# A chunk's two halves on the two halves of the partitions, back and front in one TensorE visit, and the norm on 128x512

## The chip, the core and the metric

The kernel runs on one core of a Trainium2 chip. The metric is device microseconds of one execution, the median of three. TensorE is called PE in the profile (its weight loads PEld), VectorE DVE, ScalarE ACT, GpSimd POOL, and SyncE, which issues all the DMAs, SP.

## The reference

Three layers follow one another. The first is a gated linear attention over 4 batches, 8 heads and 768 positions with a decay per position; written by chunks it is

```python
cum = np.cumsum(log_a, axis=-1)
L = np.exp(cum[..., :, None] - cum[..., None, :]) * causal
M = np.einsum('bhin,bhjn->bhij', Cc, Bc) * L          # scores with decay
y = M @ xc + (Cc @ state) * np.exp(cum)[..., None]
state = decay_full * state + sum_j(Bc x xc * decay_from_j)
```

Its output, 3072 tokens of 256 columns, goes through two MLPs. The first begins with a norm over the 256 columns, the second has no norm:

```python
rms = np.sqrt(np.mean(x * x, axis=-1, keepdims=True) + 1e-06)
xn = x / rms * rms_g
x = (silu(xn @ w_gate) * (xn @ w_val)) @ w_out        # d_ff 1536
h = x @ w_in
out = (h * np.clip(h + 3, 0, 6) / 6) @ w_out2         # d_ff 2048
```

All of it is in float32; a product of the MLPs is made of three passes over high and low parts.

## The kernel before

The time axis is cut into 24 chunks (`k`) of 128 tokens of one batch, each of two halves of 64. Four chunks make a block of 512 tokens, and there are six blocks (`j`). Phase A runs the first MLP over the blocks, 12 steps `f` for each: a step's `hidden` fills two PSUM banks (`hps`, six matmuls of 128x512 each), `gate` (ACT) and `prod` (DVE) make `p`, `gh` (ACT) and `gl` (mostly POOL) split it, and `result` adds six matmuls to `acc`. Phase B does the same for the second MLP, 16 steps for each block with one `hps` bank. Attention chunks of block j+1 and its norm are put between the steps of block j (`AT` says behind which). The first four chunks stand ahead of everything.

For a chunk, DMAs bring `cb` (its B, C and x with zeros between), `L` and `P`; DVE's scan turns `L` into the decay matrix. PE then comes three times: `score` and `grow` (`sps` at L394 and L412), later `inner` (L457 and L463), later `mean` (L482). Between them DVE makes `SM` and the states `V`, ACT the squares `sq` and the copy `xT`. `mean` sums squares with a column of ones, so that a chunk's 128 sums stand on 128 partitions; `norm` takes the inverse root of 128x4 numbers on DVE and `back` spreads them over the partitions by matmuls against `eye` (`rps`, L533). `scale` multiplies `xT` by it, and `split` makes `xh` and `xl`, which the steps read.

PSUM has eight banks: two for `acc`, and three tiles of two banks (`ps_w`, tag `w`). A step takes one such tile; a chunk holds two of them from `score` to `mean`. For the first four chunks PE spreads the decays (`spread_a`, `aps`) instead of a DMA.

No engine's order is written by hand. `Plan` collects the pieces with a cost for each engine, buffer counts and priorities, and prints a fixed order for every queue; each engine then runs its queue in that order and waits on semaphores. `P.fill` puts idle matmuls on PE in gaps of its plan before the first step.

## Time and profile before

| | before |
|---|---|
| median of three runs | 679.15 us (677.57 to 680.35) |
| profiled execution, first to last instruction | 677.3 us |
| mean granted PE clock, as a share of full speed | 0.992 |
| PE busy | 657.6 us, 97% |
| DVE, ACT, POOL busy | 301.0, 298.2, 282.7 us |

Only the span of the profiled execution is on record, not a time of its own; the median of the runs is 1.85 us above that span. Matmuls overlap, so that busy time on PE is not work at full rate.

### The profile page before, as it was taken

How to read it: one execution, taken by the hardware profiler on the slowest of the kernel's cores; microseconds unless marked ns; L12 is line 12 of the kernel's file. 1: busy time of each engine (PE TensorE's matmuls, PEld its weight loads, DVE VectorE, ACT ScalarE, POOL GpSimd, SP SyncE). 2: the span in 40 equal slices, each digit the busy share in tenths (PEclk: the TensorE clock that was granted, in tenths of full speed). 3: DMA queues.
4: the chain of work that ended last, by engine and by line, in shares of the span. 5: the costliest groups of instructions: out<-in, count | busy, mean ns of one | idle time of the engine just before them, and what ended most of it. 6: DMA issues, size and time to landing. Idle time of an engine off the chain costs nothing.

```text
span 677.3 us, 10507 instructions
## 1 busy us (share of the span) xinstructions
PE 657.6 (97%) x4188; PEld 529.0 (78%) x4188; DVE 301.0 (44%) x507; ACT 298.2 (44%) x494; POOL 282.7 (42%) x239
## 2 busy tenths in 40 slices
PE   8978999999999999999999999999999999999997
PEld 7856777778778778877867777888888888888886
DVE  4799853352234334332578773232322322332222
ACT  1576632322333223313366654445454545445543
POOL 3354453333433332432232435455454545545443
PEclk9888999999999999999999999999999999999999
DMA  5995203210221123030023420000000000000000
GB/s 196 318 320 188 95 1 95 70 55 20 91 67 44 56 65 100 1 118 1 0 94 125 142 76 0 1 0 32 1 0 32 0 32 0 1 32 0 32 0 32
DMA packets 24465, 42.92 MB, mean 63 GB/s; under 512 B 2112, under 2 KB 15712, under 8 KB 24416
## 3 DMA queue, kind: packets, MB, share of 16 engines
q1 hardware_dynamic: 24416, 42.25, 19.2%
q8 instruction: 33, 0.54, 0.3%
q14 instruction: 16, 0.13, 0.1%
HBM read 38.90 MB, written 3.34 MB: 62 GB/s over the span
## 4 chain that ended last, share of the span: by engine, by line
PE 80%; DVE 10%; ACT 3%; issue 3%; DMA 2%; POOL 1%; SPq 0%; POOLq 0%; ACTq 0%; DVEq 0%
PE hps L643 41%; PE acc L643 30%; DVE cv L608 2%; PE sps L394 2%; PE sps L463 2%; DMA L<-azero 1%; DVE cv L603 1%; DVE p L679 1%; ACT p L671 1%; PE sps L457 1%; PE sps L482 1%; DVE yT L608 1%; POOL gl L242 1%; PE sps L412 1%; PE aps L359 1%
## 5 line engine op out<-in xcount | busy, mean ns | idle before, releaser
L242 POOL TENSOR_TENSOR gl<-p,gh 128x512 fp32r<-128x512 f32 x160 | 214.3, 1341 | 239.8 <-ACT gh L686 233.1
L686 ACT CAST gh<-p 128x512 fp32r<-128x512 f32 x168 | 104.5, 622 | 94.7 <-PE acc L643 92.0
L681 DVE SCALAR_TENSOR_TENSOR p<-p,hps 128x512 f32<-128x512 f32 x96 | 65.9, 687 | 170.1 <-ACT p L673 170.1
L643 PE MATMUL hps<-xh,w1h 128*128 128x512 f32 x288 | 96.3, 416 | 7.9 <-ACT p L671 4.8
L673 ACT ACTIVATE p<-hps,half 128x512 f32<-128x512 f32 x96 | 66.3, 691 | 83.8 <-POOL gl L242 82.9
L679 DVE TENSOR_TENSOR p<-p,hps 128x512 f32<-128x512 f32 x72 | 49.3, 685 | 97.7 <-PE hps L643 75.8
L643 PE MATMUL hps<-xh,w1l 128*128 128x512 f32 x288 | 90.2, 395 | 0.0
L643 PE MATMUL hps<-xl,w1h 128*128 128x512 f32 x288 | 89.9, 393 | 0.0
L643 PE MATMUL acc<-gh,w2h 128*128 128x512 f32 x192 | 74.7, 389 | 0.0
L643 PE MATMUL acc<-gh,w2l 128*128 128x512 f32 x192 | 74.7, 389 | 0.0
L643 PE MATMUL acc<-gl,w2h 128*128 128x512 f32 x192 | 74.7, 389 | 0.0
L671 ACT ACTIVATE p<-hps 128x512 f32<-128x512 f32 x72 | 43.0, 597 | 64.6 <-POOL gl L242 33.2
L643 PEld LDWEIGHTS hps<-xh,w1h 128*128 128x128 f32 x288 | 50.0, 190 | 24.6 <-ACT p L671 8.9
L643 PEld LDWEIGHTS hps<-xh,w1l 128*128 128x128 f32 x288 | 54.6, 189 | 12.4
L643 PEld LDWEIGHTS hps<-xl,w1h 128*128 128x128 f32 x288 | 54.6, 190 | 12.3
L643 PE MATMUL hps<-xh,w2h 128*128 128x512 f32 x192 | 59.6, 391 | 1.5 <-DVE p L679 0.8
L643 PE MATMUL hps<-xl,w2h 128*128 128x512 f32 x192 | 59.2, 389 | 0.0
L643 PE MATMUL hps<-xh,w2l 128*128 128x512 f32 x192 | 59.1, 389 | 0.0
L643 PE MATMUL acc<-gh,w1h 128*128 128x512 f32 x144 | 59.0, 410 | 0.0
L643 PE MATMUL acc<-gl,w1h 128*128 128x512 f32 x144 | 56.3, 391 | 0.0
L643 PE MATMUL acc<-gh,w1l 128*128 128x512 f32 x144 | 56.2, 390 | 0.0
L242 POOL TENSOR_TENSOR bh<-cb,L 128x256 f32<-128x256 f32 x24 | 17.1, 713 | 76.4 <-PE sps L412 48.3
(94 smaller groups left out, 814.3 us busy)
## 6 DMA issues: line engine op xcount, KB each, us to landing
cb<-comb SPq DMA_DIRECT2D x20, 576.0 KB, 8.1
raw<-w SPq DMA_DIRECT2D x16, 512.0 KB, 3.4
L<-azero SPq DMA_DIRECT2D x40, 128.0 KB, 3.3
yT<-w SPq DMA_DIRECT2D x6, 768.0 KB, 9.2
rawx<-w SPq DMA_DIRECT2D x6, 768.0 KB, 9.7
...
```

Of the source, the lines that this page charges most:

```text
L242: eng[e].tensor_tensor(out=out, in0=a, in1=b, op=op)
L359: pe.matmul(out=ps[64 * q:64 * q + 64, p * CH:(p + 1) * CH], rhs=az[:, q], lhsT=eye[:96, c:c + 1].to_broadcast([96, SC]), start=True, stop ...
L394: pe.matmul(out=bank2(ws[p // 2], "sps")[:, p % 2, c * SC:(c + 1) * SC], lhsT=cb[r, BN + c * 128:BN + (c + 1) * 128], rhs=cb[r, CT + c * S ...
L412: pe.matmul(out=v()[32 * p:32 * p + 32, 1, 384 + 64 * c:448 + 64 * c], lhsT=b[:, h], rhs=cb[:, 64 * (4 * c + p):64 * (4 * c + p) + 64], st ...
L463: pe.matmul(out=o[p][c], lhsT=cb[:, q:q + 64], rhs=SM[:, p, SC * c:SC * c + SC], start=False, stop=True, skip_group_check=True)
L608: dve.scalar_tensor_tensor(out=u, in0=T[kr].bitcast(I32)[:, :, 1], scalar=-0x80000000, in1=u, op0=ALU.bitwise_and, op1=ALU.bitwise_or)
L643: pe.matmul(out=o, lhsT=a, rhs=c, start=first and i == 0, stop=last and i == len(seq) - 1)
L671: act.activation(out=p[:, :n], in_=T["w", hid][:, 0, :n], func=AF.Silu)
L673: act.activation(out=p[:, :n], in_=T["w", hid][:, 0, :n], func=AF.Relu, scale=1.0 / 6.0, bias=half)
L679: dve.tensor_tensor(out=p, in0=p, in1=h, op=ALU.mult)
L681: dve.scalar_tensor_tensor(out=p, in0=p, scalar=1.0, in1=h, op0=ALU.min, op1=ALU.mult)
L686: act.copy(out=t[:, :n], in_=T["p", i][:, :n])
```

## The change

It rewrites the attention, the norm and the places of both.

- Layout. The two halves of a chunk stand on partitions 0 to 63 and 64 to 127. `score` has a weight tile of 32 rows by 64 columns and 128 moving columns, 8 matmuls as before; `grow` one of 64 by 32; the product of `SM` and x is 16 matmuls of 64 by 32 instead of 8 of 128 by 64; the product of the state and C keeps its shape. `cb` is 896 columns wide instead of 1152.
- Visits. `visit(k)` issues `score` and `grow` of chunk k and `inner` of chunk k-1 in one piece, with a drain ahead of the state's matmuls. `decay` is one DVE instruction of 512 columns instead of two of 256; `mask` (`um`, 128x128 out of PSUM) is new, and the states are made from it.
- Squares. ACT and POOL split them into `sqh` and `sql`, and `mean` multiplies them by a 128x128 matrix of ones, so that the sums stand on all partitions: four matmuls of 128x512 for a block; `mean` for each chunk and `back` are gone. `norm` works on 128x512 in SBUF, with one ACT instruction, two for the first guess and nine Newton instructions on DVE. For the first block it works chunk by chunk on 128x128 with a root.
- PSUM. Attention has four banks of its own (`ps_at`), the hidden layer two single banks (`h`), and four (`hb`) from step 9 of block 4 on, when attention is over. Before, steps and chunks shared three pairs.
- Start. `L` of the first four chunks comes by DMA from `ablk` and is clipped on POOL; `spread_a` is gone. `P.fill` begins only behind the last of the four chunks' pieces.

Cut to its core:

```diff
-AT = {0: 0, 2: 1, 4: 2, 6: 3, 8: 4}
...
+AT = [1, 3, 5, 7]
+AT_NORM = 8
+NCB = 3
...
+        if k < B:
+            P.op(dma(262144), ld_L, w=[("L", k)], boost=bst)
+            P.op({"DVE": d2(512) + 70, "POOL": 900}, clip, r=[("L", k)], w=[("L", k)], boost=bst)
+            P.op(dma(262144), lambda e: ld_cb(e, 0, XX), w=[("cb", k, 0)], boost=bst)
+            P.op(dma(196608), lambda e: ld_cb(e, XX, CW), w=[("cb", k, 1)], boost=bst)
...
-        def spread_a(e):
-            T["aps", k] = ps = ps_acc.tile([128, 512], F32, tag="acc1", name="aps")
-            for p in range(4):
-                for q in range(2):
-                    c = 4 * k + p
-                    pe.matmul(out=ps[64 * q:64 * q + 64, p * CH:(p + 1) * CH], rhs=az[:, q],
-                              lhsT=eye[:96, c:c + 1].to_broadcast([96, SC]),
-                              start=True, stop=True, skip_group_check=True)
...
-        def score(e):
-            cb = T["cb", k]
-            for c in range(2):
-                for p in range(4):
-                    r = slice(32 * p, 32 * p + 32)
-                    pe.matmul(out=bank2(ws[p // 2], "sps")[:, p % 2, c * SC:(c + 1) * SC],
-                              lhsT=cb[r, BN + c * 128:BN + (c + 1) * 128],
-                              rhs=cb[r, CT + c * SC:CT + (c + 1) * SC],
-                              start=True, stop=True, skip_group_check=True)
...
+    def score(k):
+        cb, o = T["cb", k], part(k, 0, 128)
+        for c in range(2):
+            for p in range(4):
+                r = slice(32 * p, 32 * p + 32)
+                pe.matmul(out=o[64 * c:64 * c + 64, p],
+                          lhsT=cb[r, BN + c * SC:BN + (c + 1) * SC],
+                          rhs=cb[r, CP + c * CH:CP + (c + 1) * CH],
+                          start=True, stop=True, skip_group_check=True)
...
+    def grow(k):
+        cb, b, o = T["cb", k], flat(T["bh", k]), part(k, 192, 64)
+        for p in range(4):
+            for c in range(1 if k >= NK - B else 2):
+                r = slice(64 * c, 64 * c + 64)
+                pe.matmul(out=o[32 * p:32 * p + 32, c], lhsT=b[r, 32 * p:32 * p + 32],
+                          rhs=cb[r, XX + 64 * p:XX + 64 * p + 64],
+                          start=False, stop=True, skip_group_check=True)
...
+    def inner(k, apart=False):
+        cb, SM, y = T["cb", k], T["SM", k], part(k, 128, 64)
+
+        def intra(t):
+            for g in range(4):
+                for c in range(2):
+                    h, r = 4 * t + g, slice(64 * c, 64 * c + 64)
+                    pe.matmul(out=y[32 * g:32 * g + 32, 2 * t + c], rhs=SM[r, h],
+                              lhsT=cb[r, XX + D * h:XX + D * h + D],
+                              start=False, stop=True, skip_group_check=True)
+
+        intra(0)
+        intra(1)
+        if apart:
+            pe.drain()
+        for c in range(1 if k < B else 0, 2):
+            for p in range(4):
+                r, q = slice(32 * p, 32 * p + 32), p % 2 * 64
+                pe.matmul(out=y[q:q + 64, p // 2 * 2 + c], lhsT=before(k, c)[r, :],
+                          rhs=T["ch", k][r, SC * c:SC * c + SC],
+                          start=False, stop=True, skip_group_check=True)
...
+    def mean(o, j, cols):
+        n = 0
+        for s in ("sqh", "sql"):
             for t in range(2):
...
+                pe.matmul(out=o, lhsT=ones, rhs=T[s, j][:, t, cols], start=n == 0, stop=n == 3,
+                          skip_group_check=True)
+                n += 1
...
+        def a(e):
+            v, y, z = (t[:, cols] for t in rn(j))
+            dve.scalar_tensor_tensor(out=z, in0=v, scalar=-0.5, in1=y, op0=ALU.mult, op1=ALU.mult)
+
+        def b(e):
+            v, y, z = (t[:, cols] for t in rn(j))
+            two(e, z, z, y, ALU.mult)
+
+        def c(e):
+            v, y, z = (t[:, cols] for t in rn(j))
+            dve.scalar_tensor_tensor(out=y, in0=z, scalar=1.5, in1=y, op0=ALU.add, op1=ALU.mult)
+
+        v, y, z = keys
+        P.op({"DVE": d1(n)}, a, r=[v, y], w=[z], boost=bst)
+        P.op({"DVE": d1(n)}, b, r=[z, y], w=[z], boost=bst)
+        P.op({"DVE": d1(n)}, c, r=[z, y], w=[y], boost=bst)
...
+        P.op({"PE": 600}, lambda e: mean(m(), 0, cols),
+             r=[("sq", 0, k, 0), ("sq", 0, k, 1)], w=[s + (0,)], boost=bst)
+        P.op({"DVE": d1(128)}, shift, r=[s + (0,)], w=[v], boost=bst)
+        P.op({"ACT": a1(128)}, root, r=[v], w=[z], boost=bst)
+        P.op({"DVE": d1(128) + 100}, invert, r=[z], w=[y], boost=bst)
+        newton(0, cols, (v, y, z), None, None, bst, 128)
+        for t in range(2):
+            P.op({"DVE": d1(128)}, lambda e, t=t: scale(e, 0, t, cols),
...
+        def total(e):
+            T["h", hn] = t = mlp[1].tile([128, 512], F32, tag="h", name="rps")
+            mean(t, j, cols)
+
+        def shift(e):
+            act.activation(out=rn(j)[0], in_=T["h", hn], func=AF.Copy, scale=1.0 / DM, bias=1e-6)
...
+            v, y, z = rn(j)
+            dve.tensor_scalar(out=z.bitcast(I32), in0=v.bitcast(I32), scalar1=1, scalar2=None,
                               op0=ALU.logical_shift_right)
...
+            dve.tensor_scalar(out=y.bitcast(I32), in0=z.bitcast(I32), scalar1=-1.0,
+                              scalar2=float(0x5F3759DF), op0=ALU.mult, op1=ALU.add)
+
+        P.op({"PE": 908}, total, r=[("sq", j, i, u) for i in range(B) for u in range(2)],
+             w=[("h", hn)], boost=bst)
+        P.op({"ACT": a1(512)}, shift, r=[("h", hn)], w=[v], boost=bst)
+        P.op({"DVE": d2(512) + d1(512)}, guess, r=[v], w=[y, z], boost=bst)
+        for _ in range(3):
+            newton(j, cols, (v, y, z), None, None, bst, 512)
...
+    def open1(e):
+        early.close()
+        mlp.append(ctx.enter_context(tc.tile_pool(name="ps_acc", bufs=1, space=PSUM)))
+        mlp.append(ctx.enter_context(tc.tile_pool(name="ps_h", bufs=2, space=PSUM)))
...
     def open2(e):
         att.close()
+        mlp.append(ctx.enter_context(tc.tile_pool(name="ps_hb", bufs=4, space=PSUM, side="right")))
...
+    nstep, prev, late = [0], [], []
...
-        xk = [("x", b, t, u) for t in range(2) for u in range(2)]
-        hid, nv = nxt(nw), 2 if A else 1
+        xk, nv = xkeys[b], 2 if A else 1
+        hs = [("hb", nxt(nhb)) if late else ("h", nxt(nh)) for v in range(nv)]
...
         def hidden(e, v):
-            ps = bank2(hid, "hps")[:, v]
+            ps = hid(hs[v])
...
+    for k in range(B):
+        load(k)
+        r, w = front_keys(k)
+        free = [("xT", 0, k - 2), ("q", k - 2)] if k >= 2 else []
+        P.op({"PE": 700}, lambda e, k=k: score(k), r=r[:1] + free, w=w[:1], boost=BOOST0)
+        P.op({"PE": 500}, lambda e, k=k: grow(k), r=r + w[:1], w=w[1:], boost=BOOST0)
+        middle(k)
+        r, w = back_keys(k)
+        P.op({"PE": 1000}, lambda e, k=k: inner(k), r=r, w=w, boost=BOOST0)
+        finish_chunk(k)
+        norm_chunk(k, 0)
...
+    def visit(k):
+        new, old = k < NK, k > B
+        r, w = [], []
+        if new:
+            load(k)
+            r, w = front_keys(k)
+        if old:
+            ro, wo = back_keys(k - 1)
+            r, w = r + ro, w + wo
+
+        def go(e):
+            if new:
+                score(k)
+                grow(k)
+            if old:
+                inner(k - 1, new)
```

How it moves instructions shows in three places. The first is PE in block 1 of phase A, around one chunk; `sps` is the attention's PSUM. Before:

```order
L394 MATMUL sps<-cb 128x64 x8
L412 MATMUL sps<-cb,bh 32x64 x8
L643 MATMUL hps<-xh,w1h_77 128x512 x2
L643 MATMUL hps<-xh,w1l_89 128x512 x2
L643 MATMUL hps<-xl,w1h_77 128x512 x2
L457 MATMUL sps<-ch,V 64x64 x4
L457 MATMUL sps<-ch,V_1266 64x64 x4
L463 MATMUL sps<-SM,cb 64x64 x8
L643 MATMUL acc<-gh,w1h_83 128x512
```

And now, around a visit of the same block:

```order
L705 MATMUL acc<-gl,w1h_73 128x512
L384 MATMUL sps<-cb 64x128 x8
L395 MATMUL sps<-cb,bh 32x64 x8
L410 MATMUL sps<-SM,cb 32x64 x16
L421 MATMUL sps<-ch,V 64x64 x4
L421 MATMUL sps<-ch,V_1672 64x64 x4
L705 MATMUL acc<-gh,w1h_74 128x512
```

Before, L482's two matmuls follow five rows further down, behind the six of this `acc`. Three visits (L394 with L412, L457 with L463, L482) with MLP groups between them have become one, with 8 more matmuls of `SM`.

The second is DVE in the same block, around the norm of the next one; `z`, `y` and `v` are the norm's tiles and `rps` is PSUM. Before, the last six of eleven instructions on four columns and what follows:

```order
L525 SCALAR_TENSOR_TENSOR z_1205<-v_1203,rps 128x4
L526 TENSOR_TENSOR z_1205<-z_1205,rps 128x4
L527 SCALAR_TENSOR_TENSOR rps<-z_1205,rps 128x4
L525 SCALAR_TENSOR_TENSOR z_1205<-v_1203,rps 128x4
L526 TENSOR_TENSOR z_1205<-z_1205,rps 128x4
L527 SCALAR_TENSOR_TENSOR y_1204<-z_1205,rps 128x4
L679 TENSOR_TENSOR p<-p,hps 128x512
L539 SCALAR_TENSOR_TENSOR xT<-xT,gs,rps 128x512 x2
L248 CAST xh<-xT 128x512
L242 TENSOR_TENSOR xl<-xT,xh 128x512
```

Now, from the same place on:

```order
L519 SCALAR_TENSOR_TENSOR z_1764<-v_1762,y_1763 128x512
L234 TENSOR_TENSOR z_1764<-z_1764,y_1763 128x512
L527 SCALAR_TENSOR_TENSOR y_1763<-z_1764,y_1763 128x512
L519 SCALAR_TENSOR_TENSOR z_1764<-v_1762,y_1763 128x512
L234 TENSOR_TENSOR z_1764<-z_1764,y_1763 128x512
L746 TENSOR_TENSOR p<-p,hps 128x512
L527 SCALAR_TENSOR_TENSOR y_1763<-z_1764,y_1763 128x512
L536 SCALAR_TENSOR_TENSOR xT<-xT,gs,y_1763 128x512 x2
L441 TENSOR_TENSOR SM<-sps,L 128x512
L234 TENSOR_TENSOR xl<-xT,xh 128x512
L746 TENSOR_TENSOR p<-p,hps 128x512
```

The eleven instructions have 512 columns each, one `prod` (`p`) stands behind ten of them, and another behind `scale`, `SM` and `xl`.

The third is DVE at the start, where the weights of the first MLP (`yT` 128x768) are first put together. Before:

```order
L603 SCALAR_TENSOR_TENSOR yT<-yT 128x768
L488 TENSOR_SCALAR v_324<-sps 128x1 x2
L608 SCALAR_TENSOR_TENSOR yT<-yT 128x768
L520 RECIPROCAL rps<-rps 128x4
L525 SCALAR_TENSOR_TENSOR z_326<-v_324,rps 128x4
L526 TENSOR_TENSOR z_326<-z_326,rps 128x4
L527 SCALAR_TENSOR_TENSOR y_325<-z_326,rps 128x4
L539 SCALAR_TENSOR_TENSOR xT<-xT,gs,rps 128x512 x2
L242 TENSOR_TENSOR xl<-xT,xh 128x512
L603 SCALAR_TENSOR_TENSOR yT<-yT 128x768
```

Now:

```order
L527 SCALAR_TENSOR_TENSOR y_330<-z_331,y_330 128x128
L519 SCALAR_TENSOR_TENSOR z_331<-v_329,y_330 128x128
L536 SCALAR_TENSOR_TENSOR xT<-xT,gs,y_330 128x128
L234 TENSOR_TENSOR z_331<-z_331,y_330 128x128
L536 SCALAR_TENSOR_TENSOR xT<-xT,gs,y_330 128x128
L527 SCALAR_TENSOR_TENSOR y_330<-z_331,y_330 128x128
L536 SCALAR_TENSOR_TENSOR xT<-xT,gs,y_330 128x128 x2
L240 CAST xh<-xT 128x2x128
L234 TENSOR_TENSOR xl<-xT,xh 128x2x128
L659 SCALAR_TENSOR_TENSOR yT<-yT 128x768 x2
L664 SCALAR_TENSOR_TENSOR yT<-yT 128x768 x2
```

The first weights stood ahead of the first block's norm and stand behind its last instruction now.

## Rows read from the trace of the kernel before

**Rows 1.** The page's head and its first part, TensorE's line.

```profile
span 677.3 us, 10507 instructions
PE 657.6 (97%) x4188; PEld 529.0 (78%) x4188; DVE 301.0 (44%) x507; ACT 298.2 (44%) x494; POOL 282.7 (42%) x239
```

**Rows 2.** Line L643 alone, stretches: length, PE busy (count), granted clock, DMA share, GB/s.

```profile
31.20:60.00 28.80, 18.07 (x66) 0.94 0.95 297
60.00:84.00 24.00, 17.20 (x61) 0.93 0.35 107
209.10:271.50 62.40, 53.39 (x216) 1.00 0.20 60
333.60:410.00 76.40, 72.66 (x307) 1.00 0.28 97
410.00:677.30 267.30, 262.96 (x1159) 1.00 0.03 12
```

**Rows 3.** Stretches: length; PE, PEld, DVE, ACT, POOL busy; clock, DMA share, GB/s.

```profile
0.00:31.20 31.20, 28.08 (x371) 24.76 (x372) 18.18 (x43) 10.79 (x20) 10.50 (x22) 0.95 0.77 249
31.20:60.00 28.80, 23.84 (x209) 17.78 (x207) 27.20 (x31) 18.26 (x28) 16.57 (x12) 0.94 0.95 297
209.10:271.50 62.40, 62.29 (x498) 49.28 (x497) 23.32 (x52) 18.83 (x35) 21.89 (x21) 1.00 0.20 60
```

**Rows 4.** Timeline of PE: one chunk's two visits, later the norm's broadcast.

```profile
227.02 0.67 PE L394 MATMUL sps<-cb 32*128 32x64 f32 x16
227.62 0.43 PE L412 MATMUL sps<-cb,bh 128*32 128x64 f32 x16
227.99 0.73 PE L643 MATMUL hps<-xh,w1h 128*128 128x512 f32 x2
229.57 0.46 PE L457 MATMUL sps<-ch,V 32*64 32x64 f32 x16
229.96 0.69 PE L463 MATMUL sps<-SM,cb 128*64 128x64 f32 x16
230.57 0.50 PE L643 MATMUL acc<-gh,w1h 128*128 128x512 f32 x1
232.07 0.50 PE L482 MATMUL sps<-ones,sq 128*128 128x1 f32 x4
232.43 0.49 PE L643 MATMUL acc<-gh,w1h 128*128 128x512 f32 x1
...
270.76 1.05 PE L533 MATMUL rps<-eye,y 128*128 128x128 f32 x8
271.56 0.71 PE L643 MATMUL hps<-xh,w1h 128*128 128x512 f32 x2
```

**Rows 5.** Groups of instructions: DVE on 4 and on 256 columns.

```profile
L525 DVE SCALAR_TENSOR_TENSOR z<-v,rps 128x4 f32<-128x4 f32 x16 | 2.5, 157 | 0.5
L403 DVE TENSOR_TENSOR SM<-sps,L 128x256 f32<-128x256 f32 x48 | 18.1, 416 | 0.5 <-PE sps L394 0.4
```

**Rows 6.** Timeline of DVE, then of POOL, 340 to 346 us.

```profile
340.14 0.69 DVE L608 SCALAR_TENSOR_TENSOR cv<-raw,cv 128x512 int32<-128x512 int32 x1
...
344.33 1.73 DVE L608 SCALAR_TENSOR_TENSOR cv<-raw,cv 128x512 int32<-128x512 int32 x1
...
344.22 1.29 POOL L242 TENSOR_TENSOR w2l<-cv,w2h 128x512 fp32r<-128x512 f32 x1 [4.67 <-ACT w2h L246]
```

**Rows 7.** Timeline of PE, then of ACT: behind a group, and its gate.

```profile
259.50 0.62 PE L643 MATMUL hps<-xh,w1h 128*128 128x512 f32 x2
...
259.76 0.60 ACT L671 ACTIVATE p<-hps 128x512 f32<-128x512 f32 x1 [1.02 <-PE hps L643]
```

**Rows 8.** Timeline of the start: DVE twice, then PE.

```profile
22.88 0.95 DVE L603 SCALAR_TENSOR_TENSOR yT<-yT 128x768 int32<-128x768 int32 x1
...
29.55 0.69 DVE L242 TENSOR_TENSOR xl<-xT,xh 128x512 fp32r<-128x512 f32 x1
...
31.23 0.71 PE L643 MATMUL hps<-xh,w1h 128*128 128x512 f32 x2
```

More of the change, by code (lines that the diff above doesn't have):

```diff
@@ L156, in run @@
         if self.fill:
-            fn, ns, t, cold, until = self.fill
+            fn, ns, after, cold, until = self.fill
+            t = 1 + next(s for s, i, _, _ in out if i == after)
+            cold += t
             for s, i, _, pe in sorted(o for o in out if o[3] is not None):
@@ L399, in decay @@
-        def decay(e, t):
-            if ("SM", k) not in T:
-                T["SM", k] = ap2.tile([128, 4, CH], F32, tag="SM", name="SM")
-            q = slice(2 * t, 2 * t + 2)
-            dve.tensor_tensor(out=T["SM", k][:, q], in0=T["w", ws[t]][:, :, 0:CH], op=ALU.mult,
-                              in1=T["L", k].rearrange("j (p c) i -> j p (c i)", c=2)[:, q])
-        def grow(e):
-            cb, b = T["cb", k], T["bh", k]
-            for c in range(1 if last else 2):
-                for p in range(4):
-                    h = 2 * p + c
-                    pe.matmul(out=v()[32 * p:32 * p + 32, 1, 384 + 64 * c:448 + 64 * c],
-                              lhsT=b[:, h],
-                              rhs=cb[:, 64 * (4 * c + p):64 * (4 * c + p) + 64],
-                              start=True, stop=True, skip_group_check=True)
@@ L480, in mean @@
-        def mean(e):
-            for t in range(2):
-                pe.matmul(out=v()[:, 0, 384:385], lhsT=T["sq", j][:, t, i * CH:(i + 1) * CH],
-                          rhs=ones[:, 0:1], start=t == 0, stop=t == 1, skip_group_check=True)
-        def keep(e):
-            if ("rn", j) not in T:
-                T["rn", j] = [ap1.tile([128, B], F32, tag=n, name=n) for n in ("v0", "y0", "z0")]
-            dve.tensor_scalar(out=T["rn", j][0][:, i:i + 1], in0=v()[:, 0, 384:385],
-                              scalar1=1.0 / DM, scalar2=1e-6, op0=ALU.mult, op1=ALU.add)
@@ L491, in attention @@
-        P.op({"PE": 700 if first else 1000}, inner,
-             r=[("SM", k, 0), ("SM", k, 1), ("cb", k, 0), ("cb", k, 1), ("V1", k), ("ch", k)] + vold, w=y, boost=bst)
-        if not last:
-            P.op({"DVE": 210}, lambda e: state(e, 1), r=[("V1", k), ("P", k)] + u,
-                 w=[("V", k)], boost=BOOST)
-        P.op({"ACT": a1(256)}, square, r=y, w=[("sq", j, i)], boost=bst)
-        P.op({"ACT": a1(256), "DVE": d1(256)}, evac, r=y, w=[("xT", j, i)], boost=bst)
-        P.op({"PE": 550}, mean, r=[("sq", j, i)], w=[("w", ws[0], 4)], boost=bst)
@@ new lines, in scale, with norm_chunk @@
+    def scale(e, j, t, cols):
+        x = T["xT", j][:, t, cols]
+        dve.scalar_tensor_tensor(out=x, in0=x, scalar=gs[:, t:t + 1], in1=rn(j)[1][:, cols],
+                                 op0=ALU.mult, op1=ALU.mult)
+    def norm_chunk(k, b):
+        s, bst, cols = place(k)[0], BOOST0, slice(k * CH, k * CH + CH)
+        m = lambda: part(k, 0, 128)[:, 0]
+        v, y, z = (("rn", 0, k, n) for n in range(3))
+        def shift(e):
+            dve.tensor_scalar(out=rn(0)[0][:, cols], in0=m(), scalar1=1.0 / DM, scalar2=1e-6,
@@ L531, in back @@
-        def back(e):
-            for q in range(B):
-                pe.matmul(out=T["w", wn][:, 1, q * CH:(q + 1) * CH], start=True, stop=True,
-                          lhsT=T["rn", j][1][:, q:q + 1].to_broadcast([128, 128]),
-                          rhs=eye)
-        def scale(e, t):
-            x = T["xT", j][:, t]
-            dve.scalar_tensor_tensor(out=x, in0=x, scalar=gs[:, t:t + 1], in1=T["w", wn][:, 1],
-                                     op0=ALU.mult, op1=ALU.mult)
-        wn = nxt(nw)
@@ L747, in block_kernel @@
                 lambda f: yflat[:, 4608 + f % 2 * 768:5376 + f % 2 * 768], w1h, w1l)
+    def visit(k):
[13 more added lines that the diff above has]
+                inner(k - 1, new)
+        P.op({"PE": 1500 if new and old else 950}, go, r=r, w=w, boost=BOOST)
+        if old:
+            finish_chunk(k - 1)
+        if new:
+            middle(k)
     for j in range(NB):
```

399 lines of the change are left out of this document (205 added, 194 removed).

## Prediction

> **What bounds the kernel now.** I read the page's head first: PE is busy for 97% of the span [rows 1]. A busy PE is not a PE at its peak, so the second view is the MLP's own matmuls by stretch. In phase B they run without a break: 262.96 us for 1159 of them, 0.2269 us each [rows 2], and six of them, a group, take 1.36 us. The program has 72 steps of 18 and 96 of 12, together 2448, which is 555.5 us. The other 121.8 us of the span are what this change can touch. Three kinds of stretch hold most of them. Up to 31.2 us PE does no MLP work. From 31.2 to 84 it does 66 + 61 of these matmuls [rows 2], 28.8 us of 52.8. In a steady block, 209.1 to 271.5, the 216 matmuls need 49.0 us of 62.4, so 13.4 us are attention, norm and waiting. There are four such blocks (the attention that stands in blocks 1 to 4; that in block 0 falls in the start). From 333.6 to 410, where the second MLP's weights are prepared, 307 matmuls need 69.7 us of 76.4: 6.7 are lost. Phase B loses nothing and keeps its work.
>
> In the steady block PE is busy for 62.29 of 62.4 us, DVE for 23.32 and POOL for 21.89 [rows 3]: PE is the limit, and what leaves its queue there leaves the time. In the start DVE is: it is busy for 27.20 us of the 28.8 from 31.2 on, against 18.18 of the first 31.2 [rows 3].
>
> **PE in a steady block.** From start to start [rows 4] a chunk's first visit takes 0.97 us (227.02 to 227.99), the second 1.00 (229.57 to 230.57), `mean` 0.36, together 2.33, and the norm's `back` 0.80. Each return to the MLP costs more than its own matmuls: the group from 227.99 to 229.57 took 1.58 us instead of 1.36, the one from 230.57 to 232.07 took 1.50, so 0.18 each in the mean. 4 x 2.33 + 0.80 + 13 x 0.18 = 12.5 of the 13.4; 0.9 is waiting.
>
> What a visit costs now I take from the four kinds of matmul in [rows 4], each of 16 instructions. On four tiles of 128x32 and of 32x64 they start 23 and 24 ns apart (0.37 and 0.39 us), on two tiles of 128x64 or four of 32x128 38 ns (0.61, 0.60).
> - `score`: 16 instructions on 32x64 tiles, with twice the moving columns. 0.39 us if the columns don't count, 0.78 if they do; I take 0.50, nearer the first, since half the weight columns go.
> - `grow`: 64x32, 0.37 as now, 0.61 at worst.
> - `SM` times x: 32 instructions of 64x32, 0.77 at 24 ns, 1.22 at 38. I take 0.77, as four tiles of 32 columns do that now.
> - state times C: unchanged, 0.39.
> - the drain: no row has one. Nothing, or as much as a return with its refill, 0.22; I take 0.10.
>
> That is 2.13 us (1.92 to 3.22) instead of 2.33. Four chunks give -0.8 (-1.6 to +3.6). 13 returns become 5: -1.4. Four `mean` matmuls of 0.2269 replace `back`: +0.1. Per block -2.1 us (-2.9 to +2.3).
>
> **DVE's norm.** The eleven instructions go from 4 columns, 0.157 us [rows 5], to 512, 0.69 [rows 6]. In PE's new order two `hps` groups, `acc`, `hps`, `acc`, a visit, `acc` and three `hps` stand between the sum of squares and the next block's first step: 9 x 1.36 + 2.13 + 0.4 = 14.8 us. DVE's chain: a signal and ACT's shift 0.9 (ACT's gate begins 0.26 us behind the group's end and takes 0.60 [rows 7]), eleven of 0.69 = 7.6, one `prod` 0.7, two `scale` 1.4, `SM` 0.7, `xh` and `xl` 1.3, together 12.6 us. So it is hidden, with 2.2 us to spare. But these instructions read both inputs from SBUF, and such a one stood still while POOL worked: the one at 344.33 took 1.73 us, ending 0.55 us after a POOL subtraction that lasted from 344.22 to 345.51, against 0.69 for the one at 340.14 [rows 6]. Two `gl`, subtractions of the same size, fall within the chain and make it 15.2 or a little more. I take a wait of 0.8 us per block, with bounds of 0 and 2.6 (both subtractions in full); late next would be the block's first `hps`.
>
> The Trainium skill, "SBUF — State Buffer", section "SBUF: two separate sides", says that VectorE and GpSimd take one pair of ports as a lock for a whole instruction, and that a VectorE instruction with two SBUF inputs needs it. The 1.73 us agree; by that rule the chain would be the 15.2 us above, without it 12.6.
>
> The squares' split (ACT and POOL, 128x256) lies in those engines' idle time: 18.83 and 21.89 us of 62.4 are used [rows 3].
>
> Net, a block gains 1.3 us, four of them 5.2.
>
> **The start.** DVE gets more to do: eight `um` of some 0.3 us (between 0.157 and 0.416 [rows 5]) and four chunk norms of seven instructions at some 0.25, 9.4 us, less three of 0.69 for the old `scale` and `xl`. The cover is DVE's idle 13.0 us of the first 31.2. The old chain went through PE's `aps` and `back`, and DVE's `xl` started at 29.55 [rows 8]; four chunk norms can end sooner, at 26 to 29 by my estimate. Against it, the first weight instruction, at 22.88 before [rows 8], now stands behind the norm, some 4 us later, and block 1's norm adds 11 x 0.53 = 5.8 us on DVE at the end of the weights. PE also has no idle matmuls to keep its clock up. I take -2 us, with ends of -6 (what the chunk norms win, and fewer visits) and +5 (the weights' delay and some of the norm).
>
> **The end of phase A.** A step has four single banks in block 5 where it had three pairs; 6.7 us are lost there already. I take +0.5 (0 to +4).
>
> Sum: -5.2 - 2 + 0.5 = -6.7, a span of 670.6 us against 677.3. The median of the runs lies 1.85 above the span, which gives 672.4, so 672.
>
> **Rivals.** A difference under 0.5%, 3.4 us, is about what a measurement of this kernel can't tell from none.
> - **Waiting for two hidden banks (slower).** In phase A a step's second group may start only when the `prod` of the step before has read its bank, with one group, 1.36 us, between. `prod` needs 0.69 and the signals some 0.4 (one way 0.26 [rows 7]), so 0.3 us are to spare; one 0.69 in front of it on DVE, or one held up by POOL, costs 0.4 to 1.0. Block 1's order has some eight such pairs back to back. It decides from 1.3 us per block on, 0.17 a pair; at 0.6 a pair, 4.8 us, five blocks lose 24, less the 3.2 of norm waits that it covers: 693. Against it: while a chunk held two of the three pairs, the old steps had two banks as well, and only 0.9 us per block were lost. Chance 0.15.
> - **The norm's chain comes late.** At 2.6 us per block the blocks gain nothing: 676 to 682. For it, the 1.73 us; against it, 2.2 us to spare. Chance 0.20.
> - **The start is later.** +5 instead of -2: 679 to 684, as DVE is full from 31.2 on. Against it, its 13 idle us before. Chance 0.09.
> - **Tiles overlap further.** Two tiles gave 38 ns, four 23; with eight, 14 ns are thinkable. 80 x 0.014 = 1.1 us a visit, 1.0 less than forecast, so -16 in four blocks: 656. Against it, two kinds with different weight widths both stop at 23 to 24. Chance 0.06. The Trainium skill, "TensorE: Matmul & The Clock Gate", section "Measured speedup vs the span model", has packed tiles some 4 ns apart; no row here comes near it.
> - **More gained at the start or in the visits** (their better ends): 660 to 667. Chance 0.14.
>
> **Chances.** The forecast, 667 to 676, has 0.36. Faster by over 0.5%, below 675.8: nearly all of it, with the last two, 0.55. Within 0.5%: 0.24, from late norms and part of the late starts. Slower: 0.21, from the banks and the rest of those. The range, 659 to 686, leaves out the further overlap and about half of the banks' outcomes.
>
> **What would show it.** In the profile after: `score`'s start to the next MLP matmul, 2.1 to 2.3 us. Block to block, 60.5 to 61.5 us instead of 62.4. `xl` of the next block ending within 1 us of its first `hps`. The first `hps` of all at 29 to 33 us, 31.23 before [rows 8]. I am wrong if PE waits for `prod` by more than 2 us in a block, if `SM` times x takes 38 ns or more an instruction, or if 127 MLP matmuls are done later than at 84 us.

## The result, and the profile after

The changed kernel takes 687.69 us in the median (686.63 to 688.97, four runs), the kernel before 678.84 beside it (677.57 to 680.35): a ratio of 1.0116, interval 1.0088 to 1.0144. It is slower by 1.2%, where 672 was forecast and 659 to 686 given. The profiled execution's span is 685.5 us, 8.2 more than before. The head of its page, which answers to [rows 1]:

```profile
span 685.5 us, 11010 instructions
PE 629.9 (92%) x4398; PEld 503.5 (73%) x4398; DVE 370.4 (54%) x522; ACT 305.0 (44%) x518; POOL 310.6 (45%) x264
```

DVE is busy for 69 us more and PE for 28 less. About 15 of the 28 lie in the first 31.2 us, which the kernel before filled with idle matmuls (28.1 us busy, now 12.9). Where the time goes is seen by cutting both runs at the same work. The next two fences give the MLP's matmuls alone, in stretches that end with the 216th, the 1080th (864 more), the 1296th (216 more) and the last of them (1152 more); a count is higher by those that began ahead of the bound. The columns are those of [rows 2]. Before:

```profile
31.23:108.09 76.86, 57.15 (x217) 40.87 (x218) 0.96 0.50 157
108.09:357.82 249.73, 213.01 (x866) 157.61 (x865) 1.00 0.18 56
357.82:411.55 53.73, 51.48 (x217) 39.93 (x217) 1.00 0.30 106
411.55:677.30 265.75, 261.41 (x1152) 215.85 (x1151) 1.00 0.03 13
```

And after:

```profile
41.57:120.98 79.41, 56.79 (x217) 41.20 (x218) 0.94 0.34 115
120.98:361.09 240.11, 205.91 (x865) 162.63 (x863) 0.99 0.15 49
361.09:419.54 58.45, 51.24 (x217) 40.01 (x217) 1.00 0.34 119
419.54:685.50 265.96, 261.69 (x1152) 216.08 (x1152) 1.00 0.03 13
```

The start loses 12.9 us (the 216th matmul ends at 121.0 instead of 108.1; the first already stands 10.3 later), the four blocks win 9.6, the end of phase A loses 4.7, phase B 0.2. Forecast were -2, -5.2, +0.5 and 0.

**The blocks.** One visit, from the timeline of PE after, which answers to [rows 4]:

```profile
256.46 0.47 PE L384 MATMUL sps<-cb 32*64 32x128 f32 x16
256.87 0.34 PE L395 MATMUL sps<-cb,bh 64*32 64x64 f32 x16
257.00 0.59 PE L410 MATMUL sps<-SM,cb 64*32 64x64 f32 x32
257.70 0.46 PE L421 MATMUL sps<-ch,V 32*64 32x64 f32 x16
258.09 0.50 PE L705 MATMUL acc<-gh,w1h 128*128 128x512 f32 x1
```

From `score` to the next MLP matmul are 1.63 us. The drain stands between `SM` times x (L410) and the product of the state (L421). What it costs is seen beside the last visit, which brings no new chunk and has no drain:

```profile
329.60 0.45 PE L410 MATMUL sps<-SM,cb 64*32 64x64 f32 x32
329.98 0.46 PE L421 MATMUL sps<-ch,V 32*64 32x64 f32 x16
```

There the state's product starts 0.38 us behind the first of `SM`, in the visit with the drain 0.70. So 0.31 us of a visit come with the drain; a part may be `grow`, which stands right ahead of `SM` in the one visit and not in the other. A kernel whose visits need no drain was not tried.

In blocks 0 to 3 PE then stands still for 2.3 us, at 112.6, 174.3, 234.2 and 295.7. The timelines of DVE, POOL and PE after, at the end of the norm of the next block:

```profile
226.18 0.69 DVE L519 SCALAR_TENSOR_TENSOR z<-v,y 128x512 f32<-128x512 f32 x1
226.90 1.73 DVE L234 TENSOR_TENSOR z<-z,y 128x512 f32<-128x512 f32 x1
...
232.34 1.22 DVE L234 TENSOR_TENSOR xl<-xT,xh 128x512 fp32r<-128x512 f32 x1
233.49 0.68 DVE L746 TENSOR_TENSOR p<-p,hps 128x512 f32<-128x512 f32 x1
...
226.81 1.28 POOL L234 TENSOR_TENSOR gl<-p,gh 128x512 fp32r<-128x512 f32 x1 [1.22 <-ACT gh L753]
...
231.32 0.62 PE L705 MATMUL hps<-xl,w1h 128*128 128x512 f32 x2
234.22 0.73 PE L705 MATMUL hps<-xh,w1h 128*128 128x512 f32 x2 [2.28 <-DVE p L746]
234.78 0.97 PE L705 MATMUL hps<-xh,w1l 128*128 128x512 f32 x2
```

The `prod` at 233.49 stands behind the norm's last instructions on DVE, and PE waits 2.28 us for it. Four of the chain's instructions lie beside one of POOL and take 1.67, 1.73, 1.05 and 1.22 us (the first and third not shown) instead of 0.69. What follows the wait is slow too; two stretches of the same run, all engines, columns as in [rows 3]:

```profile
231.30:234.20 2.90, 0.64 (x3) 0.19 (x1) 2.82 (x5) 2.04 (x5) 2.48 (x2) 1.00 0.11 40
234.70:238.20 3.50, 3.50 (x11) 2.68 (x10) 1.88 (x4) 0.00 (x0) 0.38 (x1) 0.52 0.11 35
```

The granted clock is 0.52 for the 3.5 us behind the wait: PE is at the lower of its two levels for nearly all of them, and matmuls start up to 0.42 us apart instead of 0.2269. That costs another 1.6 us. So the block from 218.1 to 279.6 has 12.4 us that are not MLP: four visits 6.5, five returns 1.0, `mean` 0.9, the wait 2.3, the slow clock 1.6.

By the order of the kernel the wait needs two things: a `prod` that stands late on DVE, and a hidden layer with two banks, so that the step's second group waits for the bank which that `prod` reads. At the norm of block 5 the hidden layer already has its four banks. DVE, then PE after:

```profile
353.45 1.22 DVE L234 TENSOR_TENSOR xl<-xT,xh 128x512 fp32r<-128x512 f32 x1 [0.69 <-ACT xh L238]
354.60 0.67 DVE L746 TENSOR_TENSOR p<-p,hps 128x512 f32<-128x512 f32 x1
...
353.97 0.73 PE L705 MATMUL hps<-xh,w1h 128*128 128x512 f32 x2 [0.58 <-ACT p L738]
```

The norm's chain on DVE is 12.9 us long there (13.7 in block 2) and a `prod` stands behind it as well, but PE waits only 0.58 us, and for a gate. PE's order differs there too, so that this is a sign and not an experiment.

**The start.** The timelines of POOL, DVE, ACT and PE after:

```profile
6.21 1.91 POOL L342 TENSOR_SCALAR L<-L 128x512 f32<-128x512 f32 x1 [3.24 <-DMA L<-ablk]
...
9.64 0.41 POOL L234 TENSOR_TENSOR bh<-cb,L 128x128 f32<-128x128 f32 x1 [1.34 <-DVE L L360]
10.14 1.91 POOL L342 TENSOR_SCALAR L<-L 128x512 f32<-128x512 f32 x1
...
8.33 1.23 DVE L360 TENSOR_TENSOR_SCAN L<-L,eye 128x512 f32<-128x512 f32 x1 [4.09 <-POOL L L343]
...
37.46 0.43 DVE L234 TENSOR_TENSOR xl<-xT,xh 128x256 fp32r<-128x256 f32 x1
37.80 1.82 DVE L659 SCALAR_TENSOR_TENSOR yT<-yT 128x768 int32<-128x768 int32 x2
...
40.53 1.70 ACT L238 CAST w1h<-yT 128x768 fp32r<-128x768 f32 x2 [1.76 <-DVE yT L664]
...
41.57 0.71 PE L705 MATMUL hps<-xh,w1h 128*128 128x512 f32 x2
```

POOL's clip and DVE's scan take turns, 3.9 us a chunk, since in POOL's order a `bh`, which waits for the scan, stands ahead of the next clip. So the fourth scan starts at 19.45 us. The chunk norms end with `xl` at 37.9, where I had 26 to 29, the first weights begin there, and the first MLP matmul stands at 41.57 [rows 8: 31.23]. Later, where block 1's norm falls among the last weights, DVE after, then POOL:

```profile
93.21 0.95 DVE L659 SCALAR_TENSOR_TENSOR yT<-yT,rawx 128x768 int32<-128x768 int32 x1
...
94.94 1.51 DVE L595 TENSOR_SCALAR z<-v 128x512 int32<-128x512 int32 x1
...
104.60 0.95 DVE L664 SCALAR_TENSOR_TENSOR yT<-rawx,yT 128x768 int32<-128x768 int32 x1
...
106.49 1.82 POOL L234 TENSOR_TENSOR w1l<-yT,w1h 128x768 fp32r<-128x768 f32 x1 [3.81 <-ACT w1h L238]
```

The two halves of one conversion are 11.4 us apart, with ten instructions of the norm between them; the last weights are ready at 108.3 (87.0 before). Groups of DVE's instructions up to 121.5 us after, shapes apart, show what fills it:

```profile
L456 DVE SCALAR_TENSOR_TENSOR V<-V,P,um 128x64 f32<-128x64 f32 x14 | 9.5, 695 | 0.0
...
L527 DVE SCALAR_TENSOR_TENSOR y<-z,y 128x512 f32<-128x512 f32 x3 | 4.0, 1339 | 0.1
L536 DVE SCALAR_TENSOR_TENSOR xT<-xT,gs,y 128x512 f32<-128x512 f32 x2 | 3.9, 1981 | 0.0
L553 DVE RECIPROCAL y<-z 128x128 f32<-128x128 f32 x4 | 3.8, 949 | 0.0
L536 DVE SCALAR_TENSOR_TENSOR xT<-xT,gs,y 128x128 f32<-128x128 f32 x8 | 3.0, 402 | 0.0
```

In the kernel before, the same states up to the same work:

```profile
L425 DVE SCALAR_TENSOR_TENSOR V<-V,P,sps 128x64 f32<-128x64 f32 x14 | 3.8, 275 | 2.0 <-PE sps L463 1.0 <-ACT sq L475 0.8
```

DVE is busy for 106.2 us of the first 121.5, before for 80.1 of the first 108.4. Of the 26 more, the norms of blocks 0 and 1 are 19 (25.7 instead of 6.6, their groups together without `xh` and `xl`), the states `V` 5.7, `um` 2.6; some smaller groups have become less.

**The end of phase A.** ACT after, at the last norm and the first of the second MLP's weights (`cv`), and later at two gates (`p`):

```profile
341.19 0.60 ACT L591 ACTIVATE v<-rps 128x512 f32<-128x512 f32 x1 [0.52 <-PE rps L507]
...
352.14 1.28 ACT L238 CAST xh<-xT 128x512 fp32r<-128x512 f32 x2 [7.84 <-DVE xT L536]
356.32 0.66 ACT L651 ACTIVATE cv<-raw 128x512 f32<-128x512 f32 x1
...
376.17 0.62 ACT L238 CAST w2h<-cv 128x512 fp32r<-128x512 f32 x1 [2.02 <-DVE cv L664]
376.69 0.59 ACT L738 ACTIVATE p<-hps 128x512 f32<-128x512 f32 x1
...
394.64 0.66 ACT L651 ACTIVATE cv<-raw 128x512 f32<-128x512 f32 x1 [3.71 <-DMA raw<-w]
395.21 0.58 ACT L738 ACTIVATE p<-hps 128x512 f32<-128x512 f32 x1
```

Before, the first stood here:

```profile
338.03 0.66 ACT L595 ACTIVATE cv<-raw 128x512 f32<-128x512 f32 x1
```

These weights start when the last block's `xl` is done, 5 us ahead of the stretch's beginning instead of 20. PE's waits of over 0.3 us in the stretch are 7.0 us instead of 2.1, which is the whole loss. Two of the five are for the gates shown: 1.55 us for the one at 376.69, behind a cast that waits for DVE's `cv`, and 1.24 for the one at 395.21, behind a conversion that waits for its DMA.

### The profile page after: what moved, and what is told of

Same layout as the page of the kernel before. It is cut to its first block, busy times and chain, and to the rows that moved or that the text cites. A ratio compares the mean times of both kernels' runs of the same rounds, so it can differ in the third digit from the quotient of the medians.

```text
span 685.5 us, 11010 instructions
## 1 busy us (share of the span) xinstructions
PE 629.9 (92%) x4398; PEld 503.5 (73%) x4398; DVE 370.4 (54%) x522; ACT 305.0 (44%) x518; POOL 310.6 (45%) x264
## 4 chain that ended last, share of the span: by engine, by line
PE 68%; DVE 18%; issue 4%; ACT 4%; DMA 4%; POOL 1%; SPq 1%; DVEq 0%; ACTq 0%; POOLq 0%
PE hps L705 36%; PE acc L705 27%; DMA raw<-w 2%; DVE y L527 2%; DVE p L746 2%; DVE xT L536 2%; DVE yT L659 1%; DVE cv L659 1%; DVE cv L664 1%; DVE z L234 1%; PE sps L421 1%; DVE z L519 1%; DVE yT L664 1%; PE sps L384 1%; POOL L L342 1%
## 5 line engine op out<-in xcount | busy, mean ns | idle before, releaser
L705 PE MATMUL hps<-xh,w1h 128*128 128x512 f32 x288 | 94.4, 410 | 20.5 <-DVE p L746 15.9
L705 PE MATMUL hps<-xh,w1l 128*128 128x512 f32 x288 | 92.1, 402 | 2.8 <-POOL w1l L234 1.8
L705 PEld LDWEIGHTS hps<-xh,w1h 128*128 128x128 f32 x288 | 52.6, 192 | 38.2 <-DVE p L746 18.9
L705 PE MATMUL acc<-gh,w1h 128*128 128x512 f32 x144 | 57.0, 395 | 0.0
L705 PEld LDWEIGHTS hps<-xh,w2h 128*128 128x128 f32 x192 | 35.7, 188 | 11.8 <-ACT p L738 3.2
```

The costliest lines, as they stand in the source:

```text
L705: pe.matmul(out=o, lhsT=a, rhs=c, start=first and i == 0, stop=last and i == len(seq) - 1)
```

## The experiments

Ratios are to the kernel before, with their 95% intervals; times are medians, and the marks are from each profile, in us: the start of the first MLP matmul, the end of the 216th, and the lengths of the stretches from the 216th to the 1080th and on to the 1296th; "clock" is the mean granted clock from the first to the 216th. The expectations were written with marks read up to 1.8 us late (121.5 for the changed kernel's 216th). The runs come from several rounds, and the kernel before, 678.84 beside the changed one, took 680.1 to 681.1 beside the variants. So the ratios compare better than the times, and each row of marks is one execution.

| | us | ratio | first | clock | 216th | to 1080th | to 1296th |
|---|---|---|---|---|---|---|---|
| before | 678.84 | | 31.2 | 0.96 | 108.1 | 249.7 | 53.7 |
| changed | 687.69 | 1.0116 (1.0088 to 1.0144) | 41.6 | 0.94 | 121.0 | 240.1 | 58.5 |
| clip_dve | 685.11 | 1.0083 (1.0057 to 1.0109) | 37.7 | 0.92 | 121.0 | 240.3 | 56.4 |
| weights_first | 686.20 | 1.0096 (1.0062 to 1.0131) | 39.8 | 0.98 | 120.7 | 241.8 | 55.9 |
| six_banks | 689.11 | 1.0132 (1.0087 to 1.0176) | 42.7 | 0.89 | 122.1 | 241.2 | 57.2 |
| two_newton | 675.43 | 0.9919 (0.9892 to 0.9947) | 41.5 | 0.98 | 119.5 | 231.4 | 56.6 |
| norm_early | 682.43 | 1.0018 (0.9992 to 1.0044) | 41.3 | 0.94 | 123.7 | 236.9 | 54.7 |
| norm_early2 | 680.34 | 0.9986 (0.9967 to 1.0006) | 41.9 | 0.93 | 120.5 | 236.7 | 55.3 |
| um_psum | 689.58 | 1.0137 (1.0101 to 1.0172) | 41.4 | 0.92 | 122.3 | 242.6 | 56.4 |
| no_newton_first | 682.48 | 1.0038 (1.0016 to 1.0060) | 39.2 | 0.91 | 117.8 | 241.8 | 56.4 |
| narrow_first | 685.45 | 1.0066 (1.0039 to 1.0093) | 38.0 | 0.92 | 121.5 | 240.1 | 56.0 |
| early2_narrow | 675.76 | 0.9908 (0.9876 to 0.9941) | 35.9 | 0.94 | 117.5 | 236.4 | 54.5 |
| early2_narrow_clip | 670.47 | 0.9834 (0.9794 to 0.9874) | 35.4 | 0.95 | 111.2 | 237.6 | 54.5 |
| weights_last | 685.46 | 1.0082 (1.0053 to 1.0110) | 42.1 | 0.98 | 117.8 | 241.8 | 58.1 |
| best_weights_last | 669.86 | 0.9846 (0.9824 to 0.9868) | 34.4 | 0.93 | 110.2 | 237.6 | 55.3 |

**clip_dve.**

```diff
-            P.op({"DVE": d2(512) + 70, "POOL": 900}, clip, r=[("L", k)], w=[("L", k)], boost=bst)
+            P.op({"DVE": d2(512) + 70}, clip, r=[("L", k)], w=[("L", k)], boost=bst)
```

> The changed kernel with one edit: the first four chunks' decays are clipped on DVE instead of POOL. Theory 1 (the start is late because POOL's clip, 1.91 us, and DVE's scan take turns, 3.9 us a chunk): DVE's four scans start at 6, 8, 11 and 13 us instead of 8.3, 12.3, 16.2 and 19.5, the last sum of squares of the first block stands at 26 instead of 30.6 us, the first MLP matmul at 37 to 38 instead of 41.6, and the time falls by 3 to 5 us, to 683 to 685. Rival (DVE's own work, the four chunk norms and then the weights, sets the start, and the clip's 4 x 0.4 us come on top): the first MLP matmul stays at 41 to 42, 687 to 689.

The scans start at 6.5, 9.1, 12.8 and 15.6 us, and the first MLP matmul moves as Theory 1 has it:

```profile
37.70 0.73 PE L705 MATMUL hps<-xh,w1h 128*128 128x512 f32 x2 [1.84 <-ACT xh L238]
```

But the 216th stays at 121.0: those 3.9 us are lost again before it. The gain in the time, 2 to 3 us, is within the two intervals.

**weights_first.** The high, low, join, sign, cast and subtraction of step 0's weights (`f < 1`) get `boost=40000`.

> The changed kernel with one edit: the six instructions that make the first step's weights get a priority ahead of the first block's norm. Theory 1 (the first MLP matmul waits for weights that stand behind the whole norm on DVE: norm's last instruction ends at 37.9 us, the weight's cast at 41.5): first MLP matmul at 38.5 to 40 us, and the time falls by 1.5 to 3, to 685 to 686. Rival (DVE is full, so that 3.6 us of weights ahead of the norm push the norm by as much, or the second step's weights wait instead): first MLP matmul at 41 or later, or the gain is lost by the third step; 687 to 688.

First MLP matmul 1.8 us earlier, the 216th 0.3: the rival. Being first is not what counts in the start. In this order the last weights come earlier too, at 100.1 us instead of 108.3, and that does not help either: PE still waits 2.3 and 2.6 us, at 107.7 and 112.0, for a `prod` behind block 1's norm.

**six_banks.**

```diff
-        hs = [("hb", nxt(nhb)) if late else ("h", nxt(nh)) for v in range(nv)]
+        if late:
+            hs = [("h", nxt(nh)) if nxt(nlate) % 6 > 3 else ("hb", nxt(nhb)) for v in range(nv)]
+        else:
+            hs = [("h", nxt(nh)) for v in range(nv)]
```

> The changed kernel with one edit: from step 9 of block 4 on, the hidden layer uses the two banks of before as well as the four new ones (two of every six groups), six in all as in the kernel before. Theory (at the end of phase A PE waits 7.8 us between 353 and 423 us for gate and prod, 3.9 before, because four single banks hold two steps where three pairs held three): these waits fall to 3 to 5 us and the time by 3 to 4, to 684 to 685. Rival (the gates are late by themselves, behind ACT instructions that wait for the DMA of raw weights, so that more banks only move the wait): less than 1 us, 687 to 688.

PE's waits between 353 and 426 us are 6.2 instead of 8.1, one of them of 3.43 for a gate, and the time is the same within its interval. The rival, as far as the end of phase A goes: two more banks there do not bring its time back.

**two_newton.**

```diff
-        for _ in range(3):
+        for _ in range(2):
             newton(j, cols, (v, y, z), None, None, bst, 512)
```

> The changed kernel with two Newton iterations instead of three for the norms of blocks 1 to 5 (the third is left out, so the inverse roots are less exact): three DVE instructions of 512 columns less per block. Theory 2 (DVE's chain from the sum of squares to xl, lengthened by POOL's locks, stands ahead of a prod, and PE waits 2.3 us for it in each block, at 112.6, 174.3, 234.2 and 295.7 us): the waits of 2.3 us are gone and, with the stretches at lower clock behind two of them, the time falls by 8 to 14 us, to 674 to 680. Rival (PE waits for prod because two hidden banks leave no room, whatever DVE does): the waits stay or move, 684 to 688.

The wait of 2.3 us becomes 0.63 in blocks 2 to 4, and the clock stays at 1.00 behind it:

```profile
169.32 0.72 PE L705 MATMUL hps<-xh,w1h 128*128 128x512 f32 x2 [0.63 <-DVE p L746]
```

The four blocks take 8.7 us less, the start 1.5, the end 1.8. Theory 2, with the two hidden banks unchanged: less work on DVE in front of the `prod` is enough.

**norm_early, norm_early2.** The same theory with nothing left out.

```diff
-AT = [1, 3, 5, 7]
-AT_NORM = 8
+AT = [0, 2, 4, 6]
+AT_NORM = 7
```

> The changed kernel with the visits behind steps 0, 2, 4, 6 and the norm behind step 7 instead of 1, 3, 5, 7 and 8; nothing is left out. Theory 2 (the norm's chain on DVE starts too late, so that a prod behind it comes 2.3 us late in each block, and the second MLP's weights, which start behind the last norm, come 10 us late): one step, 4.1 us, more room takes the waits of 2.3 us away in all of the blocks, with the slow-clock stretches behind two of them, and the weights of the second MLP start some 10 us earlier than at 356; 673 to 679. Rival (the waits are for the two hidden banks and come back wherever the norm stands): 684 to 688.

For norm_early2 `AT = [0, 1, 3, 5]` and `AT_NORM = 6`.

> The changed kernel with the visits behind steps 0, 1, 3, 5 and the norm behind step 6: two steps earlier than in the changed kernel. Theory 2: as much as with one step earlier or 1 to 2 us more, since the last norm's and the second weights' start come earlier again; 671 to 678. Rival (in block 0, where DVE is full until about 112 us, visits that come earlier wait for it, and what is won in the later blocks is given back there): 680 to 688.

The waits of blocks 2 to 4 fall to 0.6 in both (norm_early2 has a second one of 0.8 for a gate), the second MLP's weights start at 350.0 and 343.6 us, and the end of phase A loses less. The times, 682.4 and 680.3, lie between theory and rival, since the start keeps its loss (and is worse by 2.7 us in norm_early). The later norm is why the changed kernel is slower in its blocks than it could be, and it is not the whole.

**um_psum.**

```diff
-            T["um", k] = t = ap2.tile([128, 2, 2 * D], F32, tag="um", name="um")
+            T["um", k] = t = part(k, 192, 64)
```

> The changed kernel with the masked growth kept in PSUM, in place, so that the states' instructions read one operand from PSUM as before the change, and with the last states of chunks 1 and 3 ahead of the opening of the MLP's banks. Theory 3 (the states' instructions, 14 of 695 ns up to 121.5 us against 275 ns before, are long because both inputs lie in SBUF and POOL works meanwhile): they fall to 250 to 300 ns, DVE has some 6 us less to do up to 121.5 us, and the time falls by 2 to 6, to 682 to 686. Rival (they are long for another reason, or DVE's load in the start doesn't matter): 695 ns stay, or the first 216 MLP matmuls end at 120 to 122 us all the same; 687 to 688.

The group of the states, up to 121.5 us:

```profile
L456 DVE SCALAR_TENSOR_TENSOR V<-V,P,sps 128x64 f32<-128x64 f32 x14 | 3.6, 271 | 0.9 <-PE sps L421 0.8
```

695 ns become 271: the cause of their length is shown. In the changed kernel the three of the fourteen that have no POOL instruction beside them take 272 to 280 ns, the longest 1818; here thirteen have one beside them, and none takes more than 281. The Trainium skill, "SBUF — State Buffer", section "SBUF: two separate sides", has this lock for a VectorE instruction with two SBUF inputs against a GpSimd one that reads SBUF; this pair of numbers agrees. The time gains nothing, though: DVE still has 104.1 us of work, and two visits wait 2.3 us each, at 68.0 and 77.6, where the changed kernel has one wait of 3.2. That they wait for the PSUM in which `um` now stands is not shown.

**no_newton_first.** `newton(0, cols, ...)` is taken out of the first block's chunk norms.

> The changed kernel with the Newton step of the first block's four chunk norms left out (the root of ACT and the reciprocal of DVE stand alone): twelve DVE instructions of 128 columns less, 5 us of DVE's time before 37 us. Theory 1 (DVE's whole work up to 112 us sets when the first 216 MLP matmuls are done, 121.5 us): they are done 3 to 5 us earlier, and the time falls by 3 to 5, to 683 to 685. Rival (what sets them is the weights' DMA or the visits' waits): the first MLP matmul comes earlier, but the 216th at 120 to 122; 687 to 688.

As Theory 1 has it: 216th at 117.8, 3.2 us earlier, and 5 us off the time.

**narrow_first, early2_narrow, early2_narrow_clip.** The first block's norm on 128x4, its core:

```diff
+                pe.matmul(out=m(), lhsT=T["q", k][:, t], rhs=ones.bitcast(F32)[:, 0:1],
+                          start=t == 0, stop=t == 1, skip_group_check=True)
...
+            pe.matmul(out=part(k, 0, 128)[:, 1], start=True, stop=True, skip_group_check=True,
+                      lhsT=rn(0)[1][:, k:k + 1].to_broadcast([128, 128]), rhs=eye)
```

> The changed kernel with one part undone: the norm of the first block on 128x4 again, with its sums by a column of ones, one root, one reciprocal, one Newton step and a broadcast by matmuls against an identity into PSUM, as in the kernel before; its scale and split stay chunk by chunk, and the later blocks keep the norm on 128x512. Theory 1 (the first block's norm on 128 columns is the DVE work that makes the start late: without its Newton step the 216th MLP matmul came 3.6 us earlier): DVE has 9 to 11 us less to do up to 121.5 us, the first MLP matmul stands at 36 to 38 instead of 41.6, the 216th at 112 to 116 instead of 121.5, and the time falls by 6 to 9, to 679 to 682. Rival (the sums come at 30.5 us as before, the weights behind them, and what DVE saves ahead of 37 us it then waits for): the 216th at 118 or later, 684 to 688.

> The first block's narrow norm together with the visits behind steps 0, 1, 3, 5 and the norm behind step 6. Theories 1 and 2 name different places, so that their gains add: 680.3 for the earlier visits alone, less 6 to 9, is 671 to 675, faster than both kernels. Rival (the earlier visits of block 0 already use the room that DVE gains): 677 to 681.

> The same, with the first four chunks' decays clipped on DVE instead of POOL. Clipping on DVE gave 3.9 us at the first MLP matmul and none at the 216th, since DVE was full behind it. Theory 1: with the norm's work gone DVE has room, and some of the 3.9 us stay: 1 to 3 us less than without, 669 to 673. Rival (DVE is still full until the weights are done): as without, 671 to 675, or 1 more for the clip's own 1.6 us.

Alone it misses: DVE's work up to 121.5 us falls from 106.2 to 98.6 us and the first MLP matmul comes at 38.0, but the 216th at 121.5; the last weights are ready at 108.9, behind block 1's norm as in the changed kernel, and PE waits 3.0 us at 113.2 for a `prod` behind that norm. With the earlier norm the 216th comes at 117.5, and the time, 675.8, lies between theory and rival. With the clip on DVE the 216th comes at 111.2 and the time falls by another 5.3 us, to the 669 to 673 of Theory 1: what gave nothing at the 216th alone gives 6.3 us here. early2_narrow_clip beats both kernels.

**weights_last, best_weights_last.** The conversions of steps 10 and 11 get `boost=30000`; the second does it in early2_narrow_clip.

> The changed kernel with one edit: the instructions for the weights of steps 10 and 11 get a priority ahead of block 1's norm. In the changed kernel's trace the last weights' second combining instruction on DVE stands behind ten instructions of that norm, at 104.6 us where the first is at 93.2, and the last weights are ready at 108.3 instead of 87.0 before the change. Theory 4 (these ten instructions, 9.7 us, are what keeps the loss of the start at 13 us whatever is won ahead of it: in all seven variants but one the 216th MLP matmul came 11 to 16 us behind the last weights): the last weights at 96 to 99, the 216th MLP matmul at 116 to 119 instead of 121.5, and the time falls by 2 to 5, to 683 to 686. Rival (the norm then ends later by what the weights take, and block 1's first step waits for its xl as long): the 216th at 120 to 122, 687 to 689.

> The fastest version so far (narrow norm for the first block, visits behind steps 0, 1, 3, 5, norm behind step 6, clip on DVE) with the weights of steps 10 and 11 ahead of block 1's norm. There the norm starts earlier against the weights, so that more of it stands ahead of them. Theory 4: 2 to 4 us less than 670.5, 666 to 669. Rival (block 1's xl is what is late, and comes later): 670 to 673.

In the first, DVE's last sign instruction stands at 95.2 instead of 104.6 us, the weights are ready at 99.0, and the 216th matmul comes at 117.8: what Theory 4 has, 3.2 of the 13 us, but its reason is not shown. The granted clock up to the 216th is 0.98 here instead of 0.94, which is worth up to 3.4 us by itself, and in weights_first the last weights at 100.1 gained nothing. The time falls by 2.2, within the intervals: the blocks, which keep their waits, take 241.8 instead of 240.1 us at a mean clock of 0.98 instead of 0.99. In early2_narrow_clip it makes no difference that the ratio shows, as the rival has it.

## Why the prediction was wrong

**The step that failed** is "The start": "I take -2 us, with ends of -6 ... and +5"; it was +12.9. Its cover was "DVE's idle 13.0 us of the first 31.2". That idle time is not room: DVE waits there for a chain of DMA, clip, scan and PE, and it had 12.2 idle of 41.5 after the change as well, 6.5 of them until a clip was done. The work I added was 13.1 us (9.4 less three of 0.69, and 5.8); measured are 26. Two parts of it were not costed: the states' operands moved from PSUM to SBUF (5.7), and of the norms' instructions, some 0.25 us for 128 columns and 0.69 for 512 in my sum, the reciprocals took 0.95, the scales 0.40 and 1.98, the last ones of a Newton step 0.40 and 1.34. Nor did I cost the new clip, 1.91 us on POOL where the plan has 0.9, in turns with the scan. And block 1's norm was seen as work "at the end of the weights", where the order put it ahead of the last of them. The idle matmuls that I missed "to keep its clock up" were no term: the granted clock is 1.00 up to 41.5 us (0.95 in the first 31.2 before), and 0.94 from there to the 216th (0.96 before).

The experiments show that this work on DVE and its place hold most of the 13 us, but no part alone does: a faster first matmul gives nothing at the 216th (clip_dve, weights_first, narrow_first), less norm work gives 1.5 and 3.2 (two_newton, no_newton_first), the last weights ahead of the norm 3.2 in weights_last and 0.3 in weights_first, and the narrow first norm, the earlier norm and the clip together 9.8. The clock of these stretches, 0.89 to 0.98, comes on top: 0.01 of it is 0.8 us, so that gains of 1 to 3 us in one profile are not told apart from it. The 2.1 us that are left in best_weights_last are not assigned.

Two of the three signs that I had set for being wrong came: PE waits over 2 us for `prod` in a block, and 127 MLP matmuls are done at 92.5 us (84.5 before).

**Right in kind, wrong in size:**
- The visit: 1.63 us instead of 2.13 (`score` 0.41 for 0.50, `grow` 0.13 for 0.37, `SM` times x with the drain 0.70 for 0.87, the states' product 0.39 as said). It gives 2.8 us per block instead of 0.8, half of what the rival of further overlap had. The 23 to 38 ns that I read from [rows 4] are means over bursts and pauses (see below), so they could not be carried over to other tiles; that the visit came out shorter in spite of the drain, 0.31 for 0.10, is because of `SM` (0.38 without it) and `grow`.
- Returns: 0.20 us each, four `mean` matmuls 0.9, as worked out.
- The norm's wait: 2.3 us instead of 0.8, with the bound of 2.6. I counted POOL's two `gl`; a `sql` and an `xl` came on top, 2.9 us in all. PE did not wait for the block's `xl` but for a `prod` queued behind it. That is the form of the rival of two hidden banks, at one place per block instead of eight. two_newton and norm_early made it short with the same banks, and at block 5's norm it is short with four. So it seems to need both, and my two rivals were halves of one. The slow clock behind it was in no term.
- Blocks together: -9.6 instead of -5.2.
- The end of phase A: +4.7, beyond the bound of 4, and two more banks do not bring it back (six_banks). In the five versions whose second weights start 11 to 14 us ahead of the stretch (norm_early and the four with the norm behind step 6) it takes 54.5 to 55.3 us; in the others, with a start 4 to 6 us ahead as in the changed kernel, 55.9 to 58.5. So the late start goes with some 1 to 3 us; the rest comes and goes with the order, and which gate it hangs on was not tried.

Of the rivals, the late start was the one that came true, beyond its price (+12.9 us, where it had +5). The late norm, with the two hidden banks, took part of what the blocks win, and the further overlap came by half; neither decided.
